# A gated linear attention and a mixer on one Trainium2 core: state parts by head pairs, shared copies, and a planner that tries 600 orders

## The chip, the core and the metric

The kernel runs on one NeuronCore of a Trainium2 chip. Its engines work side by side, each with its own queue in program order: TensorE (PE, matmuls, with weight loads as PEld), VectorE (DVE), ScalarE (ACT), GpSimd (POOL) and SyncE (SP, which only issues transfers here). They meet at semaphores. The metric is the device time of one execution in microseconds (us); the numbers shown as the time are medians of several runs. Matmuls write to PSUM, which the kernel uses as eight banks of 128 x 512 fp32; DVE and ACT read PSUM back to SBUF.

## What is computed

Inputs are q, k, v and f_logit of shape (4, 8, 768, 48) and four weight matrices. For each batch and head a 48 x 48 state is decayed by a sigmoid gate and fed by outer products of k and v; q reads it. The eight heads, side by side, are the 384 channels of a token/channel mixer.

```python
f = 1.0 / (1.0 + np.exp(-f_logit))
for t in range(S):
    state = f[:, :, t, :, None] * state + np.einsum('bhd,bhe->bhde', k[:, :, t], v[:, :, t])
    y[:, :, t] = np.einsum('bhd,bhde->bhe', q[:, :, t], state)
...
xt = x.transpose(0, 2, 1)
h = np.maximum(xt @ w_tok1, 0.0) @ w_tok2
u = x + h.transpose(0, 2, 1)
h2 = np.maximum(u @ w_ch1, 0.0) @ w_ch2
return (u + h2).astype(np.float32)
```

## The kernel before

**Tiling.** Each batch b (0 to 3) is cut into six chunks c of 128 time steps. `gates` (L318) makes, per chunk, the log of the gate on ACT (L324 to L326) and its bf16 low part Llo on DVE, or on POOL in batch 3. `attention` (L335) does a chunk:

- `sums` (L344): running sums of the logs by a triangular matmul (L352, L353), and in all but the last chunk the chunk's total per head by eight one-column matmuls (L350, L351). ACT turns them into G, Gi and glast (L361 to L367).
- DVE multiplies q by G into qh and k by Gi into kh (L369, L371). Heads are padded from 48 to 64 columns, so that two heads fill 128 rows.
- `turn` (L380, L382): eight 128 x 128 transposes into one PSUM bank; one DVE copy of 1024 elements brings them to qkT (L386).
- `scores` (L392, L396): eight matmuls, one a head, each on 48 rows of half of the array (row tiling), into two banks; DVE multiplies each bank by the triangular mask into AmT (L403).
- `parts` (L416, L419), except in the last chunk: k transposed times v for each head, eight matmuls with 64 columns of weights and 48 moving columns, of which the odd heads write to partitions 64 to 127 (column tiling). Result: 128 partitions x 4 head pairs x 48.
- The state: in chunk 0 the parts times glast (L426); later tsum = state + parts (L429) and state = tsum x glast (L431). Then two copies, one for each half of the partitions, into the block-diagonal state_bd (L434), on ACT for batches 0 to 2 and on POOL for batch 3.
- `outs` (L462): q times the earlier state (`before`, L448, four matmuls of 96 columns) and AmT times v (`within`, L455, eight of 48 columns) into one bank, copied out twice, as x_bf (bf16) and x_nat (fp32) (L470). These two go to ACT in batch 0, and to ACT or DVE otherwise.

`mixer` (L475) follows a batch: tok1 (L480), relu to h1T on ACT, tok2 (L492), DVE adds it to x_nat (L496), a bf16 copy u_bf (L501), transposes (L508) copied to uT by DVE (L513), ch1 (L524, 24 groups of three matmuls) with its relu to zT on ACT or DVE (L534, L536), and ch2 (L546, six groups of twelve) with the last DVE add (L552) and the store from SP (L555).

The copies all go through the helper `copy_on`, so they are found at L311 (ACT), L313 (DVE) and L315 (POOL). Small chunk buffers (G, Gi, qh, kh, qkT, AmT, glast, state_bd) exist twice and are taken by the parity of c.

**The order.** Nothing is emitted at once. Each step is put into a `Plan` as an operation with the engines that may run it, a rank, what it needs and makes, the PSUM bank that it uses and a cost kind. `Plan.order` (L99) is a list scheduler: it simulates the five engines with the costs of `Plan.cost` (L82), again and again takes the operation that could start first on any engine (by rank where starts are equal), fixes its engine and bank, and returns all operations by start. The kernel then emits them in that order (L584), so each engine's queue is the plan's. A matmul's cost follows its columns (`mms`, L168); the cost of scores is 270 ns and that of the state parts 210 ns, and one clock holds for the whole run. Loads keep the order in which they are added, on POOL's and SP's queues alike (`behind`); the plan models eight outstanding POOL loads, a ring of descriptors and one wire. Ranks come from `due` (L559) and `ranks` (L564).

Of the kernel before, what the change touches and what calls it, by code (L numbers as in the profile page):

```python
# [10 lines left out]
FP32 = mybir.dt.float32  # L11
# [6 lines left out]
NBANK = 8  # L18
RING = 16384


# [18 lines left out]
class Plan:  # L40
# [57 lines left out]

    def order(self):  # L99
        for op in self.ops:  # L100
            first = op.before | ({op.behind} if op.behind else set())
            op.missing = len(first)
            for x in first:
                x.after.append(op)
        free = {e: 0.0 for e in (PE, ACT, DVE, POOL, SP)}
        ready = {e: [] for e in free}
        banks = [0.0] * NBANK
        wire = 0.0
        landed: list = []
        done = []  # L110

        def offer(op):
            t = max([x.end for x in op.before], default=0.0)
            if op.kind[0] == "load" and op.engines == (POOL,) and op.kind[3]:
                if len(landed) >= 8:
                    t = max(t, landed[-8][0])
                held = op.kind[2]
                for at, rows in reversed(landed):
                    held += rows
                    if held > RING:  # L120
                        t = max(t, at)
                        break
            for e in op.engines:
                ready[e].append((t + (WAKE[e] if t else 0.0), op))

        for op in self.ops:
            if not op.missing:
                offer(op)
        while len(done) < len(self.ops):
            best = None  # L130
            for e, line in ready.items():
                for t, op in line:
                    if op.engine is not None:
                        continue
                    t = max(t, free[e])
                    if op.bank is not None and op.bank.at is None:
                        t = max(t, min(banks) + 55)
                    if best is None or (t, op.rank) < best[0]:
                        best = ((t, op.rank), e, op)
            (t, _), e, op = best  # L140
            ready[e] = [(a, o) for a, o in ready[e] if o is not op and o.engine is None]
            if op.bank is not None and op.bank.at is None:
                op.bank.at = min(range(NBANK), key=lambda j: banks[j])
                banks[op.bank.at] = math.inf
            own, till = self.cost(op, e)
            op.engine, op.start = e, t
            free[e] = t + own
            op.end = t + till
            if op.kind[0] == "load":
                size = op.kind[3]  # L150
                if size:
                    wire = max(wire, t + 1700) + size
                    op.end = wire + 1100
                if size and e == POOL:
                    landed.append((op.end, op.kind[2]))
            if op.bank is not None:
                op.bank.users -= 1
                if not op.bank.users:
                    banks[op.bank.at] = op.end
            done.append(op)  # L160
            for x in op.after:
                x.missing -= 1
                if not x.missing:
                    offer(x)
        return sorted(done, key=lambda o: o.start)

# [6 lines left out]
def kernel(  # L173
# [12 lines left out]
    nc = tc.nc  # L186
# [6 lines left out]
    DCH = moe_w_ch1.shape[1]  # L193
    NB = 3

    sb = ctx.enter_context(tc.tile_pool(name="sb", bufs=1))
    ps = ctx.enter_context(tc.tile_pool(name="ps", bufs=1, space=bass.MemoryType.PSUM))

    def st(shape, dtype, tag):
        return sb.tile(shape, dtype, tag=tag, name=tag)  # L200
# [16 lines left out]
    Llo = [st([128, NCH, H, 64], BF16, f"Llo{i}") for i in range(2)]  # L217
    G = [st([128, H, D], BF16, f"G{i}") for i in range(2)]
    Gi = [st([128, H, D], BF16, f"Gi{i}") for i in range(2)]
    qh = [st([128, H, 64], BF16, f"qh{i}") for i in range(2)]  # L220
    kh = [st([128, H, 64], BF16, f"kh{i}") for i in range(2)]
    qkT = [st([128, 8, 128], BF16, f"qkT{i}") for i in range(2)]
    AmT = [st([128, 8, 128], BF16, f"AmT{i}") for i in range(2)]
    glast = [st([128, HP], FP32, f"glast{i}") for i in range(2)]
    state = st([128, HP, D], FP32, "state")
    tsum = st([128, HP, D], FP32, "tsum")
    state_bd = [st([128, HP, 2 * D], BF16, f"state_bd{i}") for i in range(2)]

# [36 lines left out]
    def once(engine, fn, make, own):  # L265
        add(engine, 0.0, fn, make=make, kind=("fix", own, own))
# [15 lines left out]
    for i in range(2):  # L282
        for n, tl in (("L", Lhi[i]), ("L", Llo[i])):
            once(DVE, lambda tl=tl: nc.vector.memset(tl[:, :, :, D:64], 0.0), [("L", i, c) for c in range(NCH)], 400)
        for n, tl in (("qh", qh[i]), ("kh", kh[i])):
            once(DVE, lambda tl=tl: nc.vector.memset(tl[:, :, D:64], 0.0), [(n, i)], 120)
        once(DVE, lambda i=i: nc.vector.memset(state_bd[i], 0.0), [("sbd", i)], 220)
# [47 lines left out]
    def attention(b, c, r):  # L335
        i, nb = c % 2, b % NB
        last = c == NCH - 1
# [42 lines left out]
        def turn(src, o):  # L380
# [4 lines left out]
        add(PE, r, lambda: turn(kh[i], 4), need=["ident", ("kh", i)], bank=p_t, kind=mms(*[C] * 4))  # L385
        add(DVE, r, lambda: nc.vector.tensor_copy(qkT[i], turned()), make=[("qkT", i)], bank=p_t,  # L386
            kind=("el", 1024, True, 2))

# [9 lines left out]

        add(PE, r, lambda: None, need=[("qkT", i)], bank=p_a[0], kind=("mm", 1))
        two = add(PE, r, scores, need=[("qkT", i)], bank=p_a[1], kind=("mm", 270))  # L400
        plan.maker[p_a[0]] = two
# [8 lines left out]
        if not last:  # L410
            p_d = Bank()

            def dg():
                return banks[p_d.at][:, 0:HP * D].rearrange("p (hp e) -> p hp e", e=D)

            def parts():  # L416
                for h in range(H):
                    hp, par = h // 2, h % 2
                    nc.tensor.matmul(dg()[par * 64:par * 64 + 64, hp, :], lhsT=kh[i][:, h, :],  # L419
                                     rhs=v_sb[nb][:, h, c, :], start=True, stop=True)  # L420

            add(PE, r, parts, need=[("kh", i), vk], bank=p_d, kind=("mm", 210))
            gb = glast[i].unsqueeze(2).broadcast_to((128, HP, D))
            small = ("el", HP * D, True, 1)
            if c == 0:
                add(DVE, r, lambda: nc.vector.tensor_tensor(state, dg(), gb, ALU.mult),  # L426
                    need=[("glast", i)], make=["state"], bank=p_d, kind=small)
            else:
                add(DVE, r, lambda: nc.vector.tensor_tensor(tsum, state, dg(), ALU.add),  # L429
                    need=["state"], make=["tsum"], bank=p_d, kind=small)  # L430
                add(DVE, r, lambda: nc.vector.tensor_tensor(state, tsum, gb, ALU.mult),  # L431
                    need=["tsum", ("glast", i)], make=["state"], kind=small)
            for rows, cols in ((slice(0, D), slice(0, D)), (slice(64, 64 + D), slice(D, 2 * D))):
                op = add(ACT if b <= 2 else POOL, r, None, need=["state"], make=[("sbd", i, cols.start)],  # L434
                         kind=("el", HP * D, False, 1))
                op.fn = lambda op=op, rows=rows, cols=cols: copy_on(
                    op.engine, state_bd[i][rows, :, cols], state[rows])
# [7 lines left out]
        def before():  # L445
            yh = y().rearrange("t (h e) -> t h e", e=D)
            for hp in range(HP):
                nc.tensor.matmul(yh[:, 2 * hp:2 * hp + 2, :], lhsT=qkT[i][:, hp, :],  # L448
                                 rhs=state_bd[(c - 1) % 2][:, hp, :],
                                 start=(hp == 0), stop=False, skip_group_check=True)  # L450
# [8 lines left out]

        j = (c - 1) % 2  # L460

# [4 lines left out]

        past = [("qkT", i), ("sbd", j), ("sbd", j, 0), ("sbd", j, D)] if c > 0 else []
        add(PE, r, outs, need=[*past, ("AmT", i, 0), ("AmT", i, 1), vk], bank=p_y,
            kind=mms(*([96] * 4 if c else []), *[48] * 8))
        for tl, key in ((x_bf[b % 2], ("x_bf", b % 2, c)), (x_nat[b % 3], ("x_nat", b % 3, c))):  # L470
            op = add(ACT if b == 0 else (ACT, DVE), r, None, make=[key], bank=p_y, kind=el)
            op.fn = lambda op=op, tl=tl: copy_on(op.engine, tl[:, c, :], y())
# [143 lines left out]
```

## Time and profile before

| What | Value |
|---|---|
| Median of 3 runs | 188.99 us (188.82 to 189.28) |
| Profiled execution | 188.64 us, of which the span from first to last instruction 186.8 us |
| TensorE clock granted, mean by the record | 0.997 |
| L546 (ch2) | 288 matmuls, 54.1 us busy, mean 327 ns |
| L524 (ch1) | 288 matmuls, 52.6 us busy, mean 327 ns |
| L403 (mask product, DVE) | 48, 30.6 us, mean 683 ns |
| L386 (qkT copy, DVE) | 24, 16.4 us, mean 685 ns |
| L419 (state parts, PE) | 160, 6.7 us, mean 204 ns |
| L429, L431, L426 (state, DVE) | 16 of 347 ns, 16 of 353 ns, 4 of 356 ns |

Busy times on PE are of pipelined matmuls that overlap: a matmul of 384 columns is shown with 327 ns, while one starts every 162 ns or so when PE is full. The distance from one start to the next is what a matmul takes of PE's time. In a merged line of the timeline ("x4") the first number is the start of the first of them. On DVE and ACT, too, short instructions start somewhat before the one ahead has ended.

### The profile page before, as it was taken

What the parts mean: (1) busy time and instruction counts of PE and PEld (TensorE: products, weight loads), DVE (VectorE), ACT (ScalarE), POOL (GpSimd) and SP (SyncE); (2) the same over time, 40 slices, a digit from 0 to 9 for tenths busy, and PEclk for the clock granted to TensorE, in tenths of its full rate; (3) what the DMA queues carried; (4) which work ended last, traced back from release to release, by engine and by line L of the source; (5) the groups of instructions that cost most, each with busy time, mean ns of one, the idle gap of its engine ahead of it and who ended that gap; (6) DMA issues with size and microseconds to landing.
All of it is one profiled execution on the core that took longest, in us unless ns stands there. A gap on an engine that the chain in (4) does not pass through costs nothing.

```text
span 186.8 us, 4480 instructions
## 1 busy us (share of the span) xinstructions
PE 172.5 (92%) x1768; PEld 109.6 (59%) x1768; DVE 129.7 (69%) x295; ACT 126.9 (68%) x309; POOL 65.9 (35%) x78
## 2 busy tenths in 40 slices
PE   0589997799999999999999999999999999999992
PEld 0256664366667656676665665766666656656650
DVE  4387985749998999999988758977686638300222
ACT  4779963779983499999999935657875116698000
POOL 7999893275791444504621411011011000000000
PEclk9999999999999999999999999999999999999998
DMA  7999999999999999999992121011000121110222
GB/s 102 140 171 154 156 208 245 186 160 194 143 135 238 174 149 172 242 200 109 83 116 14 52 78 42 0 46 44 4 0 4 55 75 40 46 42 0 81 91 84
DMA packets 88437, 19.95 MB, mean 107 GB/s; under 512 B 81152, under 2 KB 87600, under 8 KB 88416
## 3 DMA queue, kind: packets, MB, share of 16 engines
q0 software_dynamic: 78720, 13.77, 91.9%
q1 hardware_dynamic: 9696, 5.90, 10.8%
q8 instruction: 14, 0.23, 0.5%
q14 instruction: 7, 0.06, 0.1%
HBM read 25.17 MB, written 4.72 MB: 160 GB/s over the span
## 4 chain that ended last, share of the span: by engine, by line
PE 84%; ACT 6%; DVE 3%; issue 2%; DMA 2%; POOL 1%; POOLq 0%; DVEq 0%; ACTq 0%
PE ps L524 26%; PE ps L546 24%; PE ps L382 7%; PE ps L480 5%; PE ps L396 4%; PE ps L492 3%; PE ps L455 3%; PE ps L419 3%; PE ps L352 2%; PE ps L508 2%; PE ps L353 2%; DMA f_sb<-in_f_logit_dram 2%; PE ps L448 2%; ACT u_bf L311 2%; ACT x_bf L311 1%
## 5 line engine op out<-in xcount | busy, mean ns | idle before, releaser
L546 PE MATMUL ps<-w_ch,zT 128*128 128x384 bf16 x288 | 54.1, 327 | 0.0
L524 PE MATMUL ps<-uT,w_ch 128*128 128x384 bf16 x288 | 52.6, 327 | 0.0
L534 ACT ACTIVATE zT<-ps 128x384 bf16<-128x384 f32 x76 | 36.5, 490 | 8.3 <-PE ps L524 7.9
L546 PEld LDWEIGHTS <-zT 128*128 128x128 bf16 x288 | 26.8, 98 | 16.5
L524 PEld LDWEIGHTS <-w_ch 128*128 128x128 bf16 x288 | 26.3, 97 | 15.9
L403 DVE TENSOR_TENSOR AmT<-ps,tri_bf 128x512 bf16<-128x512 f32 x48 | 30.6, 683 | 5.2 <-PE ps L396 5.0
L552 DVE TENSOR_TENSOR x_nat<-x_nat,ps 128x384 f32<-128x384 f32 x24 | 13.2, 550 | 22.9 <-PE ps L546 22.5
L255 POOL DMA_DIRECT2D q_sb<-in_q_dram x14 | 15.4, 1099 | 13.8 <-issue 5.7
L311 ACT ACTIVATE x_bf<-ps 128x384 bf16<-128x384 f32 x20 | 9.9, 494 | 12.9 <-PE ps L455 12.7
L255 POOL DMA_DIRECT2D k_sb<-in_k_dram x14 | 15.5, 1108 | 7.6 <-DMA f_sb<-in_f_logit_dram 4.5
L361 ACT ACTIVATE G<-ps 128x384 bf16<-128x384 f32 x24 | 11.7, 488 | 7.9 <-PE ps L353 7.8
L386 DVE COPY qkT<-ps 128x1024 bf16<-128x1024 bf16 x24 | 16.4, 685 | 0.8 <-PE ps L382 0.7
L255 POOL DMA_DIRECT2D v_sb<-in_v_dram x14 | 15.5, 1104 | 4.1 <-issue 2.5
L496 DVE TENSOR_TENSOR x_nat<-x_nat,ps 128x384 f32<-128x384 f32 x24 | 11.5, 548 | 4.1 <-PE ps L492 4.1
L311 ACT ACTIVATE u_bf<-x_nat 128x384 bf16<-128x384 f32 x24 | 11.4, 523 | 4.1 <-DVE x_nat L496 4.1
L315 POOL CAST state_bd<-state 48x192 bf16<-48x192 f32 x10 | 3.4, 343 | 29.8 <-DVE state L431 24.3
L324 ACT ACTIVATE f_sb<-f_sb 128x384 f32<-128x384 f32 x24 | 12.0, 523 | 2.7 <-DMA f_sb<-in_f_logit_dram 2.6
L480 PE MATMUL ps<-x_bf,w_tok 128*128 128x384 bf16 x48 | 12.3, 340 | 1.0 <-ACT x_bf L311 1.0
L536 DVE TENSOR_SCALAR zT<-ps 128x384 bf16<-128x384 f32 x20 | 10.4, 553 | 3.7 <-PE ps L524 3.6
L311 ACT ACTIVATE state_bd<-state 48x192 bf16<-48x192 f32 x30 | 10.8, 360 | 2.9 <-DVE state L431 2.6
L350 PE MATMUL ps<-ones_bf,Lhi 128*128 128x1 bf16 x80 | 7.0, 167 | 6.1 <-ACT Lhi L326 6.1
L326 ACT ACTIVATE Lhi<-f_sb 128x384 bf16<-128x384 f32 x24 | 12.2, 522 | 0.3
(58 smaller groups left out, 276.3 us busy)
## 6 DMA issues: line engine op xcount, KB each, us to landing
out_dram<-x_nat SPq DMA_DIRECT2D x24, 192.0 KB, 1.9
f_sb<-in_f_logit_dram POOLq DMA_DIRECT2D x3, 1152.0 KB, 11.0
f_sb<-in_f_logit_dram SPq DMA_DIRECT2D x6, 192.0 KB, 4.0
k_sb<-in_k_dram POOLq DMA_DIRECT2D x12, 96.0 KB, 6.3
q_sb<-in_q_dram POOLq DMA_DIRECT2D x12, 96.0 KB, 5.9
v_sb<-in_v_dram POOLq DMA_DIRECT2D x12, 96.0 KB, 6.0
w_ch<-in_moe_w_ch_dram POOLq DMA_DIRECT2D x2, 576.0 KB, 11.0
w_ch<-in_moe_w_ch_dram POOLq DMA_DIRECT2D x1, 1152.0 KB, 14.6
```

The lines of the kernel that those rows point to most:

```text
L255: add(engine, 0.0, lambda eng=eng, into=into, of=of: eng.dma_start(out=into, in_=of), make=[(n, b % NB, j) for j in (range(NCH) if c is No ...
L311: nc.scalar.activation(out_, in_, AF.Copy, bias=0.0, scale=1.0)
L324: add(ACT, r, lambda: nc.scalar.activation(fb, fb, AF.Exp, bias=0.0, scale=-1.0), make=[key], kind=el)
L326: add(ACT, r, lambda: nc.scalar.activation(hi, fb, AF.Copy, bias=0.0, scale=1.0), need=[key], make=[lk], kind=el)
L382: nc.tensor.transpose(turned()[:, o + hp, :], blk(src)[:, hp, :], ident)
L386: add(DVE, r, lambda: nc.vector.tensor_copy(qkT[i], turned()), make=[("qkT", i)], bank=p_t, kind=("el", 1024, True, 2))
L403: add(DVE, r, lambda p=p: nc.vector.tensor_tensor(AmT[i][:, 4 * p:4 * p + 4, :], banks[p_a[p].at].rearrange("s (hp t) -> s hp t", t=C), tb ...
L480: add(PE, rank("tok1", rt), lambda rt=rt, kt=kt, pm=pm: nc.tensor.matmul(banks[pm.at][:, 0:DM], lhsT=w_tok1[:, kt, rt * 128:(rt + 1) * 128 ...
L524: nc.tensor.matmul(banks[pm.at][:, 0:384], lhsT=w[:, kt, c0:c0 + 128], rhs=uT[:, kt, cols], start=(kt == 0), stop=(kt == 2))
L534: nc.scalar.activation(zT[:, cc, cols], banks[pm.at][:, 0:384], AF.Relu, bias=0.0, scale=1.0)
L546: nc.tensor.matmul(banks[pm.at][:, 0:DM], lhsT=zT[:, kt, tt * 128:(tt + 1) * 128], rhs=w_ch2[:, kt, :], start=(kt == 0), stop=(kt == 11))
L552: add(DVE, rank("ch2", tt), lambda un=un, pm=pm: nc.vector.tensor_tensor(un, un, banks[pm.at][:, 0:DM], ALU.add), make=[("x_nat", xn, tt)] ...
```

## The change

1. **State parts.** In batches 1 to 3 the eight column-tiled matmuls become four full ones, one a head pair: 128 columns of weights (both heads of kh), 96 moving columns (both heads of v). Half of each result is not wanted (one head's k with the other's v); the two wanted blocks lie on partitions 0 to 63, columns 0 to 47, and partitions 64 to 127, columns 48 to 95. So the DVE instruction that reads them (product in chunk 0, sum into tsum later) is done twice, on 64 partitions each, with its own keys in the plan. Batch 0 keeps the form by heads (`BYHEAD`).
2. **Batch 0.** The qkT copy is two halves, each on DVE or ACT (`SPLIT`); x_bf and x_nat copies may go to ACT or DVE in every batch.
3. **Buffers.** The small chunk buffers exist three times (`NI`) and are taken in turn over chunks of all batches.
4. **The plan.** A matmul group with its own tiling ("row" for scores, now 260 ns, "col" for parts by heads) is charged 105 ns whenever the tiling differs from that of the group before it (`TURN`); PE work that starts before 28 us costs 1.9 times as much and ends 180 ns later (`COLD`). `order` runs the list scheduler once with the old ranks, takes the starts found as ranks, and then tries 600 times with some ranks shifted at random (seed fixed), keeping a try whose planned end is not later. The engines, banks and order of the last one kept are used. (`slack` is defined and not called.)

```diff
+TURN = 105
+COLD = 28000
+TRIES = 600
...
+            t, _, e, k = best
+            op = self.ops[k]
+            if e == PE:
+                way = op.kind[2] if len(op.kind) > 2 else ""
+                if op.kind[1] > 1:
+                    if way != mode:
+                        t = max(t, free[PE] + TURN)
+                    mode = way
...
             own, till = self.cost(op, e)
-            op.engine, op.start = e, t
+            if e == PE and t < COLD:
+                own, till = 1.9 * own, 1.9 * own + 180
+            engine[k], start[k] = e, t
...
+        rank = [o.rank for o in self.ops]
+        found = self.attempt(rank)
+        rank, rnd = list(found[1]), random.Random(1)
+        for _ in range(TRIES):
+            far, share = rnd.choice((300, 1000, 3000)), rnd.choice((0.02, 0.1, 0.5))
+            other = [r + (rnd.gauss(0, far) if rnd.random() < share else 0) for r in rank]
+            now = self.attempt(other)
+            if now[0] <= found[0]:
+                found, rank = now, other
...
+    NI = 3
+
+    SPLIT = (0,)
+    BYHEAD = (0,)
...
-        i, nb = c % 2, b % NB
+        i, nb = (b * NCH + c) % NI, b % NB
...
-        add(DVE, r, lambda: nc.vector.tensor_copy(qkT[i], turned()), make=[("qkT", i)], bank=p_t,
-            kind=("el", 1024, True, 2))
+        for o in (slice(0, 4), slice(4, 8)) if b in SPLIT else (slice(0, 8),):
+            op = add((DVE, ACT) if b in SPLIT else DVE, r, None,
+                     make=[("qkT", i, x) for x in (0, 4) if o.start <= x < o.stop], bank=p_t,
+                     kind=("el", (o.stop - o.start) * C, True, 2))
+            op.fn = lambda op=op, o=o: copy_on(op.engine, qkT[i][:, o, :], turned()[:, o, :])
...
+                dg2 = banks[p_d.at][:, 0:DM].rearrange("p (h e) -> p h e", e=D)
+                for hp in range(HP):
+                    nc.tensor.matmul(dg2[:, 2 * hp:2 * hp + 2, :], lhsT=blk(kh[i])[:, hp, :],
+                                     rhs=v_sb[nb][:, 2 * hp:2 * hp + 2, c, :], start=True, stop=True)
...
+            add(PE, r, parts, need=[("kh", i), vk], bank=p_d,
+                kind=("mm", 210, "col") if b in BYHEAD else mms(*[2 * D] * 4))
...
+            for rows, cols, at in [both] if b in BYHEAD else halves:
+                if c == 0:
+                    add(DVE, r, lambda rows=rows, cols=cols: nc.vector.tensor_tensor(
+                        state[rows], dg(rows, cols), gb[rows], ALU.mult),
+                        need=[("glast", i)], make=[("state", x) for x in at], bank=p_d, kind=small)
+                else:
+                    add(DVE, r, lambda rows=rows, cols=cols: nc.vector.tensor_tensor(
+                        tsum[rows], state[rows], dg(rows, cols), ALU.add),
+                        need=[("state", x) for x in at], make=[("tsum", x) for x in at], bank=p_d, kind=small)
+            if c > 0:
                 add(DVE, r, lambda: nc.vector.tensor_tensor(state, tsum, gb, ALU.mult),
-                    need=["tsum", ("glast", i)], make=["state"], kind=small)
+                    need=[("tsum", 0), ("tsum", D), ("glast", i)], make=[("state", 0), ("state", D)], kind=small)
...
-            op = add(ACT if b == 0 else (ACT, DVE), r, None, make=[key], bank=p_y, kind=el)
+            op = add((ACT, DVE), r, None, make=[key], bank=p_y, kind=el)
```

## The prediction

> **What bounds the kernel now.** I read the page first: busy shares, the forty slices, and the chain of work that ended last.
>
> ```profile
> PE 172.5 (92%) x1768; PEld 109.6 (59%) x1768; DVE 129.7 (69%) x295; ACT 126.9 (68%) x309; POOL 65.9 (35%) x78
> ...
> PE   0589997799999999999999999999999999999992
> ...
> DVE  4387985749998999999988758977686638300222
> ACT  4779963779983499999999935657875116698000
> ...
> PE 84%; ACT 6%; DVE 3%; issue 2%; DMA 2%; POOL 1%; POOLq 0%; DVEq 0%; ACTq 0%
> ```
>
> TensorE (PE) carries 84% of the chain. In the slices it is full from the ninth on (one is 4.67 us); before that are two dips, at 28 to 37 us. A busy PE need not be a fast one, so next come the windows, with edges at the starts of stages (columns: stretch, its length, then busy us and instructions of PE, weight loads, DVE, ACT, POOL; clock; DMA).
>
> ```profile
> 6.00:25.00 19.00, 16.64 (x195) 10.95 (x196) 15.47 (x36) 16.80 (x47) 18.33 (x24) 1.00 2.11 164
> 25.00:38.00 13.00, 10.83 (x108) 6.59 (x106) 9.03 (x21) 7.03 (x16) 5.58 (x7) 1.00 1.35 210
> 38.00:60.00 22.00, 22.00 (x235) 14.17 (x234) 18.22 (x42) 18.20 (x47) 14.94 (x14) 1.00 1.95 173
> 60.00:100.00 40.00, 39.76 (x485) 25.69 (x483) 37.94 (x88) 36.07 (x93) 15.21 (x8) 1.00 1.91 151
> 100.00:160.00 60.00, 60.00 (x613) 38.43 (x612) 42.79 (x93) 34.14 (x81) 7.04 (x14) 1.00 0.10 34
> ```
>
> From 38 to 160 us PE idles 0.24 of 122 us: there a saved PE nanosecond is a saved nanosecond, as long as DVE and ACT keep up. They are nearly full only from 60 to 100 us, with 2.1 and 3.9 us left. Before 38 us nothing is full for long: that stage is a chain through three engines.
>
> **Part 1, state parts of batches 1 to 3.** The PE timeline of the full stage gives prices as differences of starts:
>
> ```profile
> 87.80 0.39 PE L382 MATMUL ps<-ident,qh 128*128 128x128 bf16 x4
> 88.02 1.14 PE L524 MATMUL ps<-uT,w_ch 128*128 128x384 bf16 x6
> 89.00 0.33 PE L448 MATMUL ps<-state_bd,qkT 128*128 128x96 bf16 x4
> 89.17 0.36 PE L455 MATMUL ps<-v_sb,AmT 128*128 128x48 bf16 x8
> 89.37 0.38 PE L382 MATMUL ps<-ident,kh 128*128 128x128 bf16 x4
> 89.68 0.31 PE L419 MATMUL ps<-v_sb,kh 128*64 128x48 bf16 x8
> 89.92 0.66 PE L524 MATMUL ps<-uT,w_ch 128*128 128x384 bf16 x3
> ```
>
> Four transposes (L382) take 0.22 us when a full matmul follows (87.80 to 88.02) and 0.31 when the column-tiled parts follow (89.37 to 89.68): entering the tiled form costs 0.09. The eight parts (L419) then take 0.24. The new form is four 128x96 matmuls; L448 is four such, 0.17 us. So 0.09 + 0.24 - 0.17 = 0.16 us a chunk, times 15 chunks (five in each of three batches, all after 46 us): **-2.4 us**. Bounds: -1.05 if the 0.09 stays with whatever follows (15 x 0.07), and -3.3 if the charge for turns makes half of the 18 score groups (L396; the same 0.10 at the entry) stand in pairs.
>
> The Trainium skill, TensorEngine Tiling (Array Packing), section Theoretical Speedup, speaks against this part: a small dimension of up to 64 may gain up to 2x by tiling. Eight untiled matmuls of 48 columns take 0.20 us here (L455, 89.17 to 89.37), so by that rule the tiled parts would take an estimated 0.10, and leaving them would cost 0.07 x 15 = 1.05 us, a total of 188.3. The trace shows 0.33 for them with the entry, slower than untiled; the same page, Key Properties, says that a change of mode drains the engine, which fits the 0.09. I go by the rows.
>
> In exchange the add into tsum (L429) and, in chunk 0, the product into state (L426) are done twice, on 64 partitions each. No row has such a 64-partition form; by the 128-partition one it is 0.35 us, and on POOL and ACT a 48-partition copy of the same 192 elements is not cheaper (343 and 360 ns). So 15 x 0.35 = 5.3 us more DVE, or 4.0 us by the 0.27 between starts of adjacent short DVE instructions. Cover: from 100 to 160 us DVE is idle for 17 us, and PE has the previous batch's channel matmuls to run while an attention chunk waits. From 60 to 100 us fall six of the fifteen (L419 has 48 matmuls there, eight to a chunk), 6 x 0.35 = 2.1 us, against 2.1 + 3.9 = 6.0 us free on DVE and ACT; the 20 relus that DVE takes (L536, 553 ns) can go to ACT (490 ns). Behind the second add stand the next scores' mask products and the evacuations of PSUM, and for those PE waits. Value taken: **+0.4 us**, about a tenth; bounds 0 and +5.3 (no cover at all).
>
> **Part 2, the first 38 us.** Planning costs of the old planner know one clock. The trace has two, though its clock column says 1.00 throughout: the 384-column matmul of L353 holds PE for 0.32 us at 20.85 (next start 21.17) and 0.16 at 44.46 (next 44.62). The doubling falls between 28.5 and 29.0 us.
>
> ```profile
> 26.04 1.06 PE L382 MATMUL ps<-ident,kh 128*128 128x128 bf16 x8
> 26.89 1.17 PE L480 MATMUL ps<-x_bf,w_tok 128*128 128x384 bf16 x3
> 27.99 0.61 PE L396 MATMUL ps<-qkT 48*128 48x128 bf16 x8
> 28.54 0.55 PE L480 MATMUL ps<-x_bf,w_tok 128*128 128x384 bf16 x2
> 29.02 0.40 PE L396 MATMUL ps<-qkT 48*128 48x128 bf16 x8
> ```
>
> Here three token matmuls (1.10 us) run while chunk 4's scores are nearly ready: its qkT copy began at 26.71 and takes 0.69. Two more (0.48) stand before chunk 5's scores. DVE idles 0.63 us, then runs four mask products in a row, 28.64 to 31.12, and all else of batch 0 follows them. With scores first the run starts about 0.55 us sooner, and with halves of the qkT copies on ACT (idle from 27.3 to 30.4) some 0.25 more (two whole copies take 1.29 now; three halves of 0.42, estimated below, on DVE beside one on ACT about 1.0): **-0.8**.
>
> From 33.87 DVE does six x_nat adds (2.88 us) before the first uT copy at 36.66, although three u_bf (34.45 + 3 x 0.47 = 35.9) suffice for the first half of the transposes (nine, 0.50): copies put between the adds let the first channel matmul go up to 1.4 us before its 37.75; taken **-0.5**, since the order must hit on it.
>
> From 6 to 25 us ACT and DVE are busy 32.3 of 38 us. Shared x_bf/x_nat copies, a third set of chunk buffers and cold prices in the plan can take out at most the 5.7/2 = 2.9 us; against it, splitting qkT costs a fixed part again (384 elements take 348 ns on DVE, 1024 take 685: a 512 half is about 0.42, so six splits add some 0.9 us of DVE time if both halves stay there, less on ACT). Taken **-0.5**. The memsets of the third set (0.11 + 0.11 + 0.22 us) lie in DVE's 2.8 us wait ahead of L329 at 6.06 and cost nothing; without that cover, 0.44. No load moves: POOL's and SP's loads keep their chained order, and w_ch2 (issued 32.94, 14.6 to land, so 47.6) is there before its first use at 52.5, even 3 us sooner.
>
> Start in sum: **-1.8**, bounds +1.0 (an order that fits the plan but not the chip, by the largest stalls of batch 0 now, 0.4 to 0.6 each, twice) and -4.0 (the three upper ends, 0.8 + 1.4 + 2.9, less about 1.1 for what overlaps).
>
> **Part 3, picks of 600 orders.** Inside the saturated stretch only 0.24 us idle remains to be won, so nothing is added; what the search can find is in parts 1 and 2.
>
> **Sum.** 188.64 (the profiled run: span 186.8 and 1.84 around it) - 2.4 + 0.4 - 1.8 = 184.84. The median of the runs shown is 0.35 above that execution; I add half of it: **185.0 us**.
>
> **Rivals.**
> *The start gains nothing* (the order is shorter only in the plan): for it, the early stage hangs on landing times of loads that the plan only guesses (ACT waited 2.6 us for f); against it, the misplaced token matmuls are plain to see. 188.64 - 2.4 + 0.4 + 0.2 = **186.8**. Chance 0.17.
> *The clock is released later* (ends slower). PE ran 88% busy from 6 to 25 us at half rate and doubled only after an unbroken run from 24.48 to 28.5. If the new order breaks that run, PE stays slow until the channel matmuls have run about as long. Price, doubling what lies on the chain after 28.6: 1.35 (29.02 to 30.37), 0.7 (30.95 to 31.65), 0.17, 0.32 (first tok2), 0.25 (nine transposes), and half of a 4 us run of channel matmuls, 2.0: 4.8 us. 188.64 - 2.4 + 0.4 - 1.8 + 4.8 = **189.6**. It decides once the loss passes 3.8 us, that is, a release past about 38 us. Against it: any order has this batch's PE work packed there. Chance 0.10.
> The Trainium skill, TensorE: Matmul & The Clock Gate, Part 1, puts the release after about 3.4 us of sustained work; the last run of 4 us agrees, the long busy stretch before it does not, so I lean on no date.
> *DVE becomes the bound* at 60 to 100 us: all 5.3 us paid would be 184.84 - 0.4 + 5.3 = 189.7, the half of it **187.1**; for it, 95% busy DVE; against, the room on ACT and after 100 us. Chance 0.11, of which 0.04 slower.
>
> **Chances.** Forecast 0.62 (own range 182.6 to 186.5). A change within 0.3% (0.57 us) can't be told from none. Faster 0.62 + 0.17 + 0.04 = 0.83, less 0.04 for the weak ends of these cases: 0.79. Same: 0.04 + 0.02 + 0.02 = 0.08. Slower: 0.09 (clock) + 0.04 (DVE) = 0.13. Range: low 182.2 (part 1 at -3.3 and the start at -3.5, the rest as taken), high 188.6, which takes in the first rival and half of the third.
>
> **What would show it.** Parts on four 128x96 matmuls, 0.17 from start to start, transposes before them 0.22; 15 more DVE instructions in L426/L429's places and no longer PE idle than about 0.6 us from 38 to 160; the first channel matmul near 36 us (now 37.75); spacing of 384-column matmuls halved before 30 us. I am wrong if the first channel matmul comes after 37.8, or if PE waits for DVE between 60 and 100 us by more than 2 us.

## The result: slower by 1.6%

The changed kernel takes 191.86 us (median of 4, 191.56 to 192.27) against 189.13 before (median of 4), 2.7 us more; the ratio of the runs is 1.0158, with a 95% interval of 1.0138 to 1.0178. The forecast was 185.0, with a range from 182.2 to 188.6. The profiled execution took 192.27 us with a span of 190.5, 3.6 more than before.

Page of the changed kernel: engines, slices (4.76 us each), the granted clock, the chain.

```profile
PE 172.2 (90%) x1708; PEld 109.7 (58%) x1708; DVE 139.3 (73%) x322; ACT 123.9 (65%) x305; POOL 66.7 (35%) x79
...
PE   0597869699999999989979999999999999999992
...
DVE  5369987698979979999999866998748956500222
ACT  5798973799855799899987424556791216598000
...
PEclk9999966999999999999999999999999999999998
...
PE 56%; DVE 26%; ACT 7%; issue 5%; POOL 3%; DMA 2%; DVEq 0%; POOLq 0%; ACTq 0%
```

DVE has 27 instructions and 9.6 us more, and its share of the chain that ended last went from 3% to 26%: PE now waits for it. The added adds explain 15 of the 27. Eight more are relus to zT, which the plan gave to DVE and not to ACT (20 before):

```profile
L621 DVE TENSOR_SCALAR zT<-ps 128x384 bf16<-128x384 f32 x28 | 14.9, 555 | 2.6 <-PE ps L609 2.6
```

The windows (stretch, length, busy us and instructions of PE, weight loads, DVE, ACT, POOL) say where:

```profile
38.00:60.00 22.00, 21.80 (x216) 14.30 (x217) 20.30 (x48) 17.61 (x46) 14.92 (x14) 1.00 1.94 173
60.00:100.00 40.00, 37.47 (x432) 24.37 (x430) 38.56 (x88) 35.73 (x94) 17.11 (x11) 1.00 1.96 150
100.00:160.00 60.00, 59.93 (x610) 38.99 (x609) 45.86 (x102) 29.80 (x73) 5.38 (x12) 1.00 0.10 34
```

From 60 to 100 us PE issues 432 matmuls where it issued 485, and idles 2.5 us where it idled 0.24. Of the 53 fewer, 24 are the new form itself (24 matmuls at L491 where 48 stood) and 21 are channel matmuls (51 at L609, 72 at L524 before): these are the work that came later. DVE is hardly busier there than before (38.56 to 37.94): it was full, and the work that no longer fits is late. The new matmul form itself does what was forecast. In the timeline of PE:

```profile
58.66 0.39 PE L446 MATMUL ps<-ident,qkh 128*128 128x128 bf16 x4
58.88 0.33 PE L491 MATMUL ps<-v_sb,qkh 128*128 128x96 bf16 x4
59.05 0.81 PE L631 MATMUL ps<-w_ch,zT 128*128 128x384 bf16 x4
```

Transposes 0.22 us from start to start (58.66 to 58.88), parts 0.17 (to 59.05).

To split the time of every kernel I use three numbers of its trace. **Start**: when the first channel matmul begins (37.75 us before, 39.30 after). **Stalls**: after that, the distance between starts on PE beyond what the matmul takes when PE is full (162 ns for 384 columns, 56 for 128, 42 for 96, 25 for 48), where it exceeds 50 ns. **Turns**: up to 110 ns for each change between full and tiled matmuls, taken out of the stalls. Before: stalls 0.9, turns 6.5 us. After: stalls 5.6, turns 3.7. So 2.8 us were won at turns, 4.7 lost in stalls, and the start is 1.55 later. The sums of stalls and turns are good to about 0.4 us, since they hang on the price taken for each matmul. One caution: in the five kernels that keep the order before (it, E1, E2, E3, E17) the start lies between 37.75 and 38.84 us, so starts less than 1.1 us apart say nothing.

### The profile page after: what moved, and what is told of

Its sections match the earlier page's. It is cut to its first block, busy times and chain, and to the rows that moved or that the text cites. A ratio compares the mean times of both kernels' runs of the same rounds, so it can differ in the third digit from the quotient of the medians.

```text
span 190.5 us, 4357 instructions
## 1 busy us (share of the span) xinstructions
PE 172.2 (90%) x1708; PEld 109.7 (58%) x1708; DVE 139.3 (73%) x322; ACT 123.9 (65%) x305; POOL 66.7 (35%) x79
## 4 chain that ended last, share of the span: by engine, by line
PE 56%; DVE 26%; ACT 7%; issue 5%; POOL 3%; DMA 2%; DVEq 0%; POOLq 0%; ACTq 0%
PE ps L609 21%; PE ps L631 18%; DVE AmT L471 6%; PE ps L565 4%; DVE tsum L512 3%; DVE qkT L377 3%; PE ps L446 3%; DVE state L516 2%; PE ps L577 2%; DMA f_sb<-in_f_logit_dram 2%; DVE x_nat L637 2%; PE ps L463 2%; PE ps L540 2%; ACT u_bf L375 1%; DVE x_nat L581 1%
## 5 line engine op out<-in xcount | busy, mean ns | idle before, releaser
L631 PE MATMUL ps<-w_ch,zT 128*128 128x384 bf16 x288 | 54.7, 326 | 0.0
L609 PE MATMUL ps<-uT,w_ch 128*128 128x384 bf16 x288 | 51.7, 326 | 0.3 <-DVE zT L621 0.2
L609 PEld LDWEIGHTS <-w_ch 128*128 128x128 bf16 x288 | 26.9, 98 | 16.8 <-issue 0.2
L619 ACT ACTIVATE zT<-ps 128x384 bf16<-128x384 f32 x68 | 31.9, 492 | 6.1 <-PE ps L609 5.7
L446 PE MATMUL ps<-ident,qkh 128*128 128x128 bf16 x192 | 20.7, 238 | 1.3 <-DVE qkh L433 1.2
L446 PEld LDWEIGHTS <-qkh 128*128 128x128 bf16 x192 | 14.1, 105 | 7.5 <-DVE qkh L433 3.6
L621 DVE TENSOR_SCALAR zT<-ps 128x384 bf16<-128x384 f32 x28 | 14.9, 555 | 2.6 <-PE ps L609 2.6
L377 DVE COPY qkT<-ps 128x1024 bf16<-128x1024 bf16 (+1 forms) x24 | 14.7, 616 | 0.7 <-ACT qkT L375 0.4
L375 ACT ACTIVATE x_nat<-ps 128x384 f32<-128x384 f32 x13 | 6.3, 488 | 12.6 <-PE ps L540 8.0
L565 PE MATMUL ps<-x_bf,w_tok 128*128 128x384 bf16 x48 | 14.0, 354 | 0.2 <-ACT x_bf L375 0.2
L375 ACT ACTIVATE x_bf<-ps 128x384 bf16<-128x384 f32 x16 | 7.6, 489 | 9.4 <-PE ps L540 7.8
```

Of the source, the lines that this page charges most:

```text
L375: nc.scalar.activation(out_, in_, AF.Copy, bias=0.0, scale=1.0)
L377: nc.vector.tensor_copy(out_, in_)
L446: nc.tensor.transpose(turned()[:, o + hp, :], blk(src)[:, hp, :], ident)
L565: add(PE, rank("tok1", rt), lambda rt=rt, kt=kt, pm=pm: nc.tensor.matmul(banks[pm.at][:, 0:DM], lhsT=w_tok1[:, kt, rt * 128:(rt + 1) * 128 ...
L609: nc.tensor.matmul(banks[pm.at][:, 0:384], lhsT=w[:, kt, c0:c0 + 128], rhs=uT[:, kt, cols], start=(kt == 0), stop=(kt == 2))
L619: nc.scalar.activation(zT[:, cc, cols], banks[pm.at][:, 0:384], AF.Relu, bias=0.0, scale=1.0)
```

## The experiments

**The state parts, with the queue order of the kernel before frozen.** The plan is the old one; only what a step issues differs. E1 has the four matmuls and one add, and so leaves out the odd heads' own parts of the state; E2 has the doubled adds (parts by heads), E3 both.

```diff
-                for h in range(H):
-                    nc.tensor.matmul(dg()[par * 64:par * 64 + 64, hp, :], lhsT=kh[i][:, h, :], ...)
+                for hp in range(HP):
+                    nc.tensor.matmul(dg2[:, 2 * hp:2 * hp + 2, :], lhsT=blk(kh[i])[:, hp, :], ...)
...
+                for rw, cl in halves:
+                    nc.vector.tensor_tensor(tsum[rw], state[rw], dg(rw, cl), ALU.add)
```

> The kernel before with its queue order frozen; in batches 1 to 3 the state parts are four 128x96 matmuls, and the add reads one 128-partition block, so the odd heads' half of the state takes the unwanted block. DVE's work is as before. Theory A (the matmul form saves PE time, the loss is elsewhere): 2.4 us less, about 186.6. Rival B (the saving is eaten because the next engine sets the pace): within 0.6 us of before, 188.5 to 189.6.

> Order frozen as before, parts by heads as before, but each add into tsum and each chunk-0 product of batches 1 to 3 is issued as two instructions of 64 partitions: 15 more DVE instructions and nothing else. Theory C (the doubled DVE work is the cost): 3 to 5 us more, 192 to 194. Rival D (DVE has room, the loss comes from the order): at most 1 us more, under 190.1.

> Order frozen as before, head-pair parts and doubled adds together: the state part of the change without any replanning, a full computation. If parts and adds simply add up: E1's and E2's differences summed. By A with D about 187.2, faster than before; by A with C 189.5 to 191.5.

E1: 187.92 us, ratio 0.9947 (0.9911 to 0.9983): 1.2 us by the medians, half of the 2.4, and by the interval 0.3 to 1.7. It lies between A's number and B's. Turns fall by 2.8 us, stalls grow by 1.1. E2: 194.00, ratio 1.0274 (1.0217 to 1.0332), 4.9 us for 15 short instructions. E3: 193.33, ratio 1.0233 (1.0173 to 1.0294), about the sum of the two (+3.7). Theory C holds, and D falls: in this order almost nothing hides the adds. PE's and DVE's timelines of E2 show one place:

```profile
61.20 0.71 DVE L434 TENSOR_TENSOR tsum<-state,ps 64x192 f32<-64x192 f32 x2
61.94 0.36 DVE L442 TENSOR_TENSOR state<-tsum,glast 128x192 f32<-128x192 f32 x1
62.33 0.69 DVE L386 COPY qkT<-ps 128x1024 bf16<-128x1024 bf16 x1
62.94 0.70 DVE L434 TENSOR_TENSOR tsum<-state,ps 64x192 f32<-64x192 f32 x2
63.67 0.56 DVE L563 TENSOR_TENSOR x_nat<-x_nat,ps 128x384 f32<-128x384 f32 x1
64.14 0.68 DVE L386 COPY qkT<-ps 128x1024 bf16<-128x1024 bf16 x1
```

```profile
63.08 0.40 PE L396 MATMUL ps<-qkT 48*128 48x128 bf16 x8
64.89 0.40 PE L396 MATMUL ps<-qkT 48*128 48x128 bf16 x8 [0.78 <-DVE qkT L386]
```

Two pairs of adds (x2) stand in the queue before the qkT copy at 64.14 for which PE's next scores wait: 0.78 us of idle PE. The windows of E2 show the lag:

```profile
60.00:100.00 40.00, 38.65 (x480) 24.68 (x477) 38.49 (x89) 32.97 (x84) 15.08 (x8) 1.00 1.84 155
100.00:150.00 50.00, 48.78 (x528) 30.95 (x527) 39.31 (x87) 33.32 (x80) 7.04 (x14) 1.00 0.18 31
```

DVE gains half a microsecond from 60 to 100 us, ACT loses 3 us (32.97 against 36.07); I read this as work that waits for DVE's results. And from 100 to 150 us PE idles 1.2 us although DVE has 11 us free.

**The planner and its prices.** E4 takes both new charges out of the changed kernel, E7 the search.

```diff
-TURN = 105
-COLD = 28000
+TURN = 0
+COLD = 0
...
-TRIES = 600
+TRIES = 0
```

> The changed kernel with the two new charges of the plan set to nothing (no price for a change of tiling, full clock from the start), the search of 600 orders kept. Theory E (the order made with the new prices is the loss, since it lets DVE and ACT run just in time for a PE that the old prices hurried): 186 to 188. Rival F (prices do not matter, what counts is the added work): 191 to 193.

> The changed kernel without the 600 tries: the first order is used. The plan's own end is 186.6 against 184.4 us. If the search's gain is real on the chip: 194, 2.1 us more than the changed kernel. If it is a gain on paper alone: within 0.8 us of it.

E4: 191.09 us, ratio 1.0103 (1.0042 to 1.0163), at the low end of F's numbers and 3 us above E's; its interval meets that of the changed kernel. E7: 197.26, ratio 1.0399 (1.0346 to 1.0452): the search is worth about 5 us on the chip (5.4 by the medians, 4.6 by the ratios), more than the 2.1 of the plan. What it searches from is bad.

**One part of the change undone.** E5 has `BYHEAD = (0, 1, 2, 3)`, E8 `(0, 1, 2)`; E6 goes back to two buffer sets, whole qkT copies and batch 0's copies on ACT.

```diff
-    NI = 3
-    SPLIT = (0,)
+    NI = 2
+    SPLIT = ()
...
-            op = add((ACT, DVE), r, None, make=[key], bank=p_y, kind=el)
+            op = add(ACT if b == 0 else (ACT, DVE), r, None, make=[key], bank=p_y, kind=el)
```

> The changed kernel with the state parts of all batches by heads again, as before; sharing, third buffers, new prices and the search kept. Theory C (the doubled adds are the whole loss): 187 to 188.5, at least 3 us under the changed kernel. Theory G (the rest of the change, which moves more copies to DVE and makes orders that run late, loses too): 190 or more. The plan's own end is 186.4 us for this one and 184.4 for the changed kernel, so the plan expects 2 us the other way.

> The changed kernel with two sets of chunk buffers, whole qkT copies on DVE and batch 0's x copies on ACT, as before; state parts by pairs, new prices and search kept. The plan's own end is 183.4 us against 184.4. Theory H (sharing puts work on DVE that it has no room for and gives the greedy planner bad choices): 1 to 3 us under the changed kernel, 189 to 190.9. Rival C (sharing is neutral): within 0.8 us of it, 191 to 192.6.

> The changed kernel with head pairs in batch 3 alone, where DVE had idle time: 5 chunks. Theory C: two thirds of the doubled adds are gone and the rest is covered, so 1 to 3 us under the changed kernel and at or below the form by heads (E5) by up to 0.8. Theory G: no better than E5.

E5: 194.57 us, ratio 1.0270 (1.0228 to 1.0312). Theory C as I had it, the adds as the whole loss, falls: without the pairs the rest of the change is slower still, as the plan had said. E8: 193.59, ratio 1.0228 (1.0188 to 1.0268), in between; C had put it under the changed kernel. E6: 190.49, ratio 1.0057 (1.0019 to 1.0094): H holds. E6 starts at 36.49 us, the changed kernel at 39.30.

**The planner alone, on the work of the kernel before.** E9 has both prices and the search, E10 the search alone, E11 the cold price and the search; E12 is E10 with pairs.

> The kernel before in all its work (parts by heads, two buffer sets, whole qkT copies, batch 0's copies on ACT), ordered by the new planner with both new prices and 600 tries; the plan's end is 186.2 us. Theory E (orders made with the new prices are worse on the chip than the old one): 191 to 193. Rival H (prices and search are sound, sharing and buffers do the harm): 187 to 189.

> As the one before it, but without the two new prices; the plan's end is 178.6 us, against 178.2 for the order before. Theory E: 188 to 189.5, about the time before. Rival H: no better than with the prices, within 0.8 us of it.

> As E9 with the price for the half clock and none for a change of tiling; the plan's end is 180.5 us. If the loss of E9 against E10 is due to the charge for tiling (it overstates: 260 ns and two turns of 105 for a score group that takes 0.42 us with its entry): at E10's time. If it is due to the cold price: at E9's time.

> State parts by pairs in batches 1 to 3, no sharing, two buffer sets, old prices, search kept; the plan's end is 180.4 us. Against E6 (the same with the new prices, 190.5): Theory E gives 189 to 190 or less; theory C says that no order hides the doubled adds, 191 or more.

| Kernel | us | ratio (95%) | start | stalls |
|---|---|---|---|---|
| E10 search, old prices | 188.89 | 0.9982 (0.9956 to 1.0008) | 36.8 | 2.8 |
| E11 and the cold price | 190.67 | 1.0078 (1.0044 to 1.0113) | 37.6 | 3.6 |
| E9 and the charge for turns | 191.20 | 1.0121 (1.0067 to 1.0175) | 37.2 | 4.1 |
| E12 E10 with pairs | 189.94 | 1.0053 (1.0023 to 1.0083) | 38.1 | 6.5 |

New orders for the same work: one as good as before, two worse, as theory E had said for E9 and E10. E11 against E10 puts most of that loss with the cold price; what the charge for turns adds (E9) is within the intervals. The cold price should have mended the early stage, but E11's start is no earlier than E10's, and its stalls are 0.8 us longer. With pairs the prices make no clear difference: E12 against E6, and E4 against the changed kernel, are 0.6 and 0.8 us faster, and their intervals meet. So theory E holds by half. The three orders of the same work stall some 2 to 3 us longer than the order before.

Start and stalls are those of the one profiled execution. For E12 it took 192.33 us, 2.4 over the median, so its 6.5 us of stalls is too high for the kernel's usual run. In that execution the pairs take 2.6 us off the turns against E10 and put 3.7 into the stalls.

Each setting was ordered with one seed. A new price, buffer or choice of engine gives another order altogether, and no run here orders one setting twice. What these rows lay to a price may therefore in part be the luck of one order; that is not tested.

**What makes the start late, and whether the plan lacks reserve.** E13, E14 and E15 add one of E6's three removals again; E16 is E6 with `1.06 *` on DVE's and ACT's costs in the plan.

> E6 (pairs, new planner, two buffer sets, whole qkT copies) with batch 0's x_bf and x_nat copies on ACT or DVE. If the greedy plan puts x_nat copies, which nothing waits for, in front of the qh, kh and qkT work of DVE: the first channel matmul 1 to 2.5 us later than E6's 36.5 us, and 191 to 192.5 in all. If sharing helps the start as forecast: at 36.5 or earlier.

> E6 with batch 0's qkT copies in two halves on DVE or ACT, nothing else. If the halves are the cost (0.42 us on DVE and 0.61 on ACT for what takes 0.69 whole, and two may land on one engine): first channel matmul 0.5 to 1.5 us later than E6's 36.5. If they help as forecast: up to 0.25 earlier.

> E6 with three sets of chunk buffers, nothing else. If a third set lets early chunks run ahead and pushes the last ones of batch 0 back: first channel matmul 0.5 to 1.5 us later than E6's 36.5. If it only removes waits: at 36.5 or earlier and the time at or under E6's 190.5.

> E6 with every DVE and ACT instruction 6% longer in the plan alone; the plan's own end is 187.2 us against 183.4. If the stalls of 60 to 100 us (5.6 us of PE time in E6) come of an order that leaves no reserve: 2 us or more of them go, 188 to 189. If the engines lack the time itself: within 0.8 us of E6's 190.5.

E13: start 40.47, 195.24 us, ratio 1.0327 (1.0306 to 1.0347). E14: 38.28, 192.87, ratio 1.0197 (1.0177 to 1.0217). E15: 37.91, 192.10, ratio 1.0151 (1.0123 to 1.0179). Each alone is worse than E6, sharing most, and by more than was expected (4.0 us of start for 1 to 2.5). They do not add up: alone they cost 4.8, 2.4 and 1.6 us over E6, all three together in the changed kernel 1.4. DVE's timeline of E13, at the end of batch 0:

```profile
25.80 0.35 DVE L516 TENSOR_TENSOR state<-tsum,glast 128x192 f32<-128x192 f32 x1
26.07 0.55 DVE L377 COPY x_nat<-ps 128x384 f32<-128x384 f32 x1
26.54 0.54 DVE L377 CAST x_bf<-ps 128x384 bf16<-128x384 f32 x1
27.00 0.35 DVE L433 TENSOR_TENSOR qkh<-q_sb,G 128x384 bf16<-128x384 bf16 x1
27.27 1.28 DVE L471 TENSOR_TENSOR AmT<-ps,tri_bf 128x512 bf16<-128x512 f32 x2
...
30.05 0.55 DVE L377 CAST x_bf<-ps 128x384 bf16<-128x384 f32 x1
30.52 0.68 DVE L377 COPY qkT<-ps 128x1024 bf16<-128x1024 bf16 x1
31.12 2.47 DVE L471 TENSOR_TENSOR AmT<-ps,tri_bf 128x512 bf16<-128x512 f32 x4
```

and E6's, where ACT does those copies:

```profile
25.84 0.68 DVE L377 COPY qkT<-ps 128x1024 bf16<-128x1024 bf16 x1
26.44 0.35 DVE L516 TENSOR_TENSOR state<-tsum,glast 128x192 f32<-128x192 f32 x1
27.07 0.69 DVE L377 COPY qkT<-ps 128x1024 bf16<-128x1024 bf16 x1 [0.28 <-PE ps L446]
27.68 2.47 DVE L471 TENSOR_TENSOR AmT<-ps,tri_bf 128x512 bf16<-128x512 f32 x4
```

The last four mask products, behind which the rest of batch 0 hangs, begin at 27.68 in E6 and at 31.12 in E13. An x_nat copy, for which nothing waits yet, stands in front of the qh product (27.00) and the qkT copies: the plan takes what can start first. From 22.34 to 29.20 us DVE (third of the busy times) has no gap left, while ACT (fourth), which did these copies in E6, is busy little more than half of the time:

```profile
22.34:29.20 6.86, 6.59 (x79) 4.70 (x79) 6.86 (x17) 3.98 (x11) 6.33 (x6) 1.00 1.22 205
```

The clock has a share that these runs do not separate: eight scores took 0.54 us from start to start at 29.60 in E13, 0.33 at 27.91 in E6, so E13 was at half clock for longer (the clock column says 1.00 here, as it did for the half clock of the kernel before).

E16: 194.05 us, ratio 1.0257 (1.0227 to 1.0286), stalls 9.5, of which 7.4 lie between 60 and 100 us. Of these, 2.4 go with one wait for a load of v, and 1.0 with a stretch at half clock that follows it (last section); some 4.0 are left against E6's 5.6. Two us or more were expected to go. So the forecast for reserve fails, but on one order with a mishap of its own.

**Pairs where DVE pays nothing.** E17 and E18 take pairs in batch 3 alone and give that batch's product of tsum and glast to GpSimd.

```diff
-                add(DVE, r, lambda: nc.vector.tensor_tensor(state, tsum, gb, ALU.mult),
+                add(DVE, r, lambda: (nc.gpsimd if b == 3 else nc.vector).tensor_tensor(state, tsum, gb, ALU.mult),
```

> The order before, frozen; head pairs and doubled adds in batch 3 alone, and batch 3's product of tsum and glast on GpSimd, so that DVE gains five adds and loses four products. If the matmul form is worth 0.16 us a chunk once DVE pays nothing: 5 x 0.16 = 0.8 us less, 188.4. If the state chain's longer step on GpSimd comes late for the queue's order: 189 to 190.

> The same work as E17, ordered by the new planner with the old prices and 600 tries, without sharing or third buffers. By E10 (188.9) less 0.8: 188.1. If every replanned order stalls alike between 60 and 100 us: 189 or more.

E17: 188.89 us, ratio 0.9975 (0.9951 to 0.9999), 0.4 us of the 0.8, and too near 1 to be called a gain. E18: 191.65, ratio 1.0132 (1.0092 to 1.0173); this new order loses more than the form wins. No kernel here that computes the reference beats the one before by more than that.

## Why the prediction was wrong

**What bounds the kernel** was read rightly, but from the wrong side. PE was full, so I took each PE nanosecond as won. What kept it full was an order in which DVE and ACT, 95% and 90% busy from 60 to 100 us, brought each result in time: E10 lengthens stalls by 1.9 us with no other work at all. Of the two signs of being wrong that the prediction named, the first came plainly (first channel matmul at 39.30 us, after 37.8), the second at its edge: PE idled 2.5 us from 60 to 100, 2.0 of them by the trace's waits for DVE.

**Part 1, PE.** The rows after show the priced forms: 0.17 us, and no entry. In E1 turns fell by 2.8 us, a little more than the -2.4 forecast. The kernel got 1.2 of it (0.3 to 1.7 by the interval), so the term's mechanism was right, and about half of its size arrived.

**Part 1, DVE: the step that failed first.** "Value taken: +0.4 us, about a tenth; bounds 0 and +5.3". E2 measured +4.9, near the far bound. The price of an add was right (349 ns for 64 partitions, by L512 of the changed kernel). Nearly all of it was paid where I had it covered nine parts in ten. The cover was wrong: I compared sums of free time over windows, and engine time that is free in some gap is no cover for an instruction that stands in a queue in front of one that PE waits for. The free 17 us after 100 us did not help either: E2 stalls there too. Nor did relus make room by going to ACT: DVE takes 28 where it took 20. How much of the changed kernel's own 4.7 us of added stalls is due to the adds is not shown: E9, with no added work, stalls 3.2 us longer than the order before, and a new order may hide much of the adds (E6 and the changed kernel are under E3).

**Part 2, the start: the step that failed with the wrong sign.** Forecast -1.8, measured +1.55 in the profiled runs. That lies outside my bounds too (-4.0 to +1.0). The first two terms (scores ahead of token matmuls; uT copies earlier; together -1.3) come out in E6, whose first channel matmul is 1.26 us sooner than before, at the edge of the scatter. But that the sum fits so well is luck. Second token matmuls and first channel matmul of the kernel before, of E6 and of the changed kernel:

```profile
33.12 2.33 PE L492 MATMUL ps<-h1T,w_tok 128*128 128x384 bf16 x12 [0.41 <-ACT h1T L484]
37.75 0.65 PE L524 MATMUL ps<-uT,w_ch 128*128 128x384 bf16 x3
...
32.03 2.33 PE L577 MATMUL ps<-h1T,w_tok 128*128 128x384 bf16 x12 [0.42 <-ACT h1T L569]
36.49 0.65 PE L609 MATMUL ps<-uT,w_ch 128*128 128x384 bf16 x3
...
34.61 2.33 PE L577 MATMUL ps<-h1T,w_tok 128*128 128x384 bf16 x12 [0.41 <-ACT h1T L569]
39.30 0.98 PE L609 MATMUL ps<-uT,w_ch 128*128 128x384 bf16 x5
```

Up to the second token matmuls E6 wins 1.09 us (0.8 forecast; its clock was up for good at 27.4 us, before at 28.7), from there to the first channel matmul 0.17 of the 0.5. The changed kernel loses 1.49 of its 1.55 before the second token matmuls, in batch 0's attention. The third, "taken -0.5" for shared copies, split qkT and a third set, is where it failed: E6 to the changed kernel is +2.8 us of start. I had bounded it by idle time of the engines and had named only the cost of halves and memsets. What a greedy planner does with one more choice I did not ask; E13 shows one such order.

**Part 3, the search** was put at nothing, because PE had only 0.24 us idle to win. It had about 5 us to repair (E7): the first order of the changed plan was far worse than the order before. That the plan is no worse than its first try was no comfort, since that first try was not the order before. That the order itself could lose was in no term: E9, the same work in a new order, has a ratio of 1.0121, some 2 us.

**The rivals.** DVE as the bound came nearest, and its price of 5.3 us was near E2's; I gave it 0.11, and let it start from a sum that held a start gain. The late clock did not happen as priced: the clock was released earlier (21.9 us), fell back to half from 25.4 to 32.2, and so was up for good 3.5 us later than before (28.7). Two executions of this kernel at a mean clock of 0.979 and 1.000 differ by 0.7 us (192.27 and 191.56), a quarter of the loss. E17, which keeps the old order and batch 0's work, had such a fall too (22.3 to 29.2 us) and took 188.50, so the fall is not peculiar to the change. "The start gains nothing" held for the start, but with the adds unpaid it gave 186.8.

**How the loss adds up** along one path of medians, each step being one order: search alone 188.9, with both prices 191.2 (E9), with pairs 190.5 (E6), with sharing, halves and the third set 191.9. Along other paths the same part has another price: the pairs are +4.2 us in the frozen order, +1.1 (E10 to E12), -0.7 (E9 to E6) and -2.7 (E5 to the changed kernel). Why the order before stalls so little is open: its plan ends at 178.2 us by the old prices, E10's at 178.6, and a difference that small says nothing, since with the new prices plans that end at 186.2 (E9) and 186.4 (E5) have spans of 188.9 and 193.1.

## What to carry to other kernels

A saving on a full engine counts only if the engines that feed it keep their places in time: price added work by what stands behind it in its queue, and take the full cost unless the trace shows the gap that swallows it at that place. More choices for a greedy planner can make it slower; compare its new order with the old one on the same work first, and do not rank orders by the planner's own end.

## What the runs showed of the hardware

**DVE blocked by GpSimd.** In the changed kernel two of the products of tsum and glast, 353 ns in the kernel before, took 853 and 1068 ns. The timelines of DVE and GpSimd:

```profile
89.01 0.85 DVE L516 TENSOR_TENSOR state<-tsum,glast 128x192 f32<-128x192 f32 x1
...
87.85 1.79 POOL L396 TENSOR_TENSOR Llo<-f_sb,Lhi 128x384 bf16<-128x384 f32 x2 [2.39 <-ACT Lhi L390]
```

GpSimd runs batch 3's Llo subtraction until 89.64 us, and the product ends at 89.86. In E6 one took 1466 ns beside two such subtractions. The kernel before had none of these delays. The Trainium skill, SBUF — State Buffer, section SBUF: two separate sides, says that a DVE instruction with two SBUF inputs and a GpSimd instruction that reads SBUF exclude each other for the whole instruction; these rows agree. The delays cost the changed kernel 1.2 us of DVE time in its full stretch. The plan's costs know of no such delay, so any new order can meet it: one product took 930 ns in E10, one 1070 in E11.

**The clock can be given and taken back.** In the changed kernel the clock was up from 21.9 us and fell back at 25.4. In these 3.4 us PE idled 0.31 and 0.26 us, and a gap of 1.46 us (a wait for mask products) had begun at 24.60. E17 fell back after gaps of 0.33 us at most. Its windows show the granted clock behind the five busy times:

```profile
18.93:22.34 3.41, 2.38 (x45) 1.60 (x43) 3.41 (x8) 3.34 (x10) 3.00 (x5) 1.00 2.35 148
22.34:29.20 6.86, 6.48 (x59) 3.99 (x59) 5.72 (x14) 4.18 (x12) 6.12 (x6) 0.50 1.20 206
```

PE idled 1.03 of the 3.41 us there. In E16 a gap of 2.21 us on PE before 80.18 stands ahead of a fall from 81.5 to 84.9 us. What share of idle time brings the fall is not shown. The Trainium skill, TensorE: Matmul & The Clock Gate, Part 1, tells of a fall after an idle window of about 3.4 us; here E17's window, in which PE was idle for under a third of the time, preceded one.
